# A kernel that streams weights through a ring: four places instead of five, one more weight pair on chip, and two PSUM accumulators instead of three

## The chip, the core and the metric

The kernel runs on one core of a Trainium2 chip. Its work is spread over engines with queues of their own: TensorE (PE; PEld are its weight loads), VectorE (DVE), ScalarE (ACT), GpSimd (POOL) and SyncE (SP, which here only issues DMAs). Each engine takes its instructions in the order in which the program gives them, and waits at an instruction until the semaphores that it needs have come. SBUF is the memory on chip that operands are read from, PSUM the one that TensorE writes its results to, and DRAM lies off chip. The metric is the device time of one execution in microseconds (us); lower is better.

## The reference

Two independent results stand side by side in the output. The first is a convolution layer (`A`); it is done in the kernel's first stages, which the change leaves alone. The second (`B`) is a recurrence over 64 segments of 32 tokens. Eight memory rows are carried from one segment to the next, so that no segment can begin before the one ahead of it has ended:

```python
for s in range(n_seg):                                   # 64 segments, seg_len 32
    xs = x[:, s * seg_len:(s + 1) * seg_len, :]
    h = jnp.concatenate([mem, xs], axis=1)               # 8 + 32 rows of 1024
    q = jnp.einsum('btd,dhe->bhte', h, Wq)               # 32 heads of 128
    k = jnp.einsum('btd,dhe->bhte', h, Wk)
    v = jnp.einsum('btd,dhe->bhte', h, Wv)
    scores = jnp.einsum('bhqe,bhke->bhqk', q, k) * scale
    p = _softmax(jnp.where(mask, scores, -1e9), axis=-1)
    o = jnp.einsum('bhqk,bhke->bhqe', p, v)
    o = jnp.einsum('bhte,hed->btd', o, Wo)
    mem = o[:, :M, :]                                    # M = 8
    outs.append(o[:, M:, :])
```

Each of `Wq`, `Wk`, `Wv`, `Wo` has 1024 x 4096 numbers of two bytes, so every segment uses 32 MB of weights.

## The kernel before

**Weight pairs.** The weights are cut into 64 pairs; a pair is a tile of 128 partitions x 2 x 1024 bf16, 512 KB or 4 KB in each partition. `("qk", g, kc)` holds rows 128 kc and on of `Wq` and `Wk` for the eight heads of group g (32 pairs), `("v", G, kc)` those of `Wv` for sixteen heads (16 pairs), and `("o", g, i)` two heads of `Wo` (16 pairs). They are kept in three ways, which `STREAM` (line 40) and `PARKED` (line 41) lay down. 45 pairs are resident in SBUF. 17 are streamed: each step fetches them from DRAM anew, into a ring of `RING` = 5 places of one pair each (line 697). Two are parked: they stay in PSUM, one tile of 128 x 1024 bf16 (2 KB in each partition) for each half pair (`park`, lines 669 and 670), and each step copies them into a place of the ring.

**The ring.** `done(key)` (line 725) is called when a streamed pair's last matmul has been issued. It takes the place for the next streamed pair in the order of use and issues that load on SP's queue (`place`, line 708). After the pairs that are keys of `PARKED` it gives the place to a parked pair instead, and `unpark` (line 716) copies that pair's first half with ACT (line 719) and its second half with DVE (line 720). `unpark` is called twice in a step: after the first half of group 0's q/k projection, and after group 0's transposes. A load of a pair waits for the matmuls that last read the place, and the loads behind it on SP's queue wait with it.

**One step.** The loop over 64 segments (line 908) is written out by hand, and this order is that of every engine's queue. Four groups u0 to u3 of eight heads go through these parts:

- `qk_part`: 32 matmuls accumulate q and k of one group, eight pairs with four matmuls each, into one PSUM tile of 128 x 512 fp32. `qk_out` (line 757) lets ACT cast it to `qks`.
- `tr_a` (line 783): four transposes on PE, then two ACT copies and one POOL copy to `QK`.
- `scores` (line 806): 20 small matmuls, then two DVE operations. `softmax` (line 828): two exponentials on ACT, then four DVE operations. `blocks` (line 845): four copies to `PB`, on DVE ("D") or ACT ("A").
- `v_part` (line 761): 32 matmuls for sixteen heads into `vacc`; `v_out` (line 772) is an ACT cast.
- `pv` (line 854): four matmuls into `otacc`; ACT casts the 32 rows of the segment to `OT` (line 863), DVE the other eight columns to `OL` (line 865).
- `wo` (line 869): 32 matmuls of one group into `Y`, which all four groups share.

`qkacc`, `vacc`, `otacc` and `yacc` are all tiles of the pool `ps_a` with three buffers (line 701): an accumulator waits for whoever read the one three before it. With the four park tiles, and one tile of `ps_ts` for the transposes and the scores, eight PSUM tiles of 2 KB in each partition are in use.

At the end of a step ACT casts `Y` (line 985), PE transposes its memory rows, and DVE writes them into the next `hT`, which every projection of the next step reads. POOL stores the outputs and loads the next `VB`.

**Order around the change.** Groups 2 and 3 go as follows (lines 944 to 970): the second half of u2's projection and its cast; `pv` of u0; `blocks` of u1; the first two pairs of u3's projection; u2's transposes; four more pairs; u2's scores and softmax; the last two pairs and the cast; then, in turns, one pair of v's second half, `pv` of u1, `blocks` of u2, one pair of v, u3's transposes, three pairs of v, u3's scores, softmax, the last three pairs of v, the cast of v, and `wo` of u0.

**Ahead of the loop** the resident pairs are loaded during the convolution stages, as SBUF comes free, the streamed q/k and output pairs are copied in DRAM into the shape of a pair (`relay`), and the parked halves are brought into PSUM through two rounds of transposes (lines 669 to 692). Nine output pairs are loaded in the first step (`first_loads`). In the last step the streamed output pairs are loaded once more, into places of resident pairs that are no longer needed (line 940). After the loop, four long accumulations (`pl`, line 1003) work out the outputs of the last eight rows of all segments.

Of the kernel before, what the change touches and what calls it, by code (L numbers as in the profile page):

```python
# [9 lines left out]
BF = mybir.dt.bfloat16  # L10
F32 = mybir.dt.float32
# [4 lines left out]
PSUM = bass.MemoryType.PSUM  # L16
# [5 lines left out]
def fused_kernel(ctx: ExitStack, tc, q, k, v, shift_k, ssm_k, ssm_D, outa, x, mem0, Wq, Wk, Wv, Wo, outb, n_seg):  # L22
# [11 lines left out]
    nc = tc.nc  # L34
# [3 lines left out]
    scale = 128.0 ** -0.5  # L38
    RING = 5
    STREAM = {"qk": ((2, 5), (3,), (2, 6), (2, 6)), "v": ((0, 3, 5), (1, 5)), "o": ((2,), (1,), (0, 3), (2,))}  # L40
    PARKED = {("qk", 0, 2): ("v", 0, 1), ("v", 0, 3): ("qk", 1, 6)}

    msched = tc.manual_schedule()
# [624 lines left out]

    ps_park = cw_.enter_context(tc.tile_pool(name="b_ps_park", bufs=1, space=PSUM))
    park = {key: [ps_park.tile([128, 1024], BF, name=f"park{key[1]}_{n}") for n in range(2)] for key in parked}  # L670

    park_s = stv.tile([128, 4, 1024], BF, tag="stv", name="park_s")
    halves = [(key, n) for key in parked for n in range(2)]
    assert rows.at >= 160
# [10 lines left out]
    for i, (key, n) in enumerate(halves):  # L685
        tw = ps_p.tile([128, 1024], BF, tag="pp", name="park_t")
        for c in range(8):
            nc.tensor.transpose(tw[:, c * 128:(c + 1) * 128], park_w[i][:, c * 128:(c + 1) * 128], ident[:])
        nc.vector.tensor_copy(park_s[:, i, :], tw[:])
        rows.half(2, "AD")  # L690
        for c in range(8):
            nc.tensor.transpose(park[key][n][:, c * 128:(c + 1) * 128], park_s[:, i, c * 128:(c + 1) * 128], ident[:])
    while rows.at < 192:
# [6 lines left out]
    pp = ExitStack()  # L700
    ps_a = pp.enter_context(tc.tile_pool(name="b_ps_a", bufs=3, space=PSUM))
    ps_ts = pp.enter_context(tc.tile_pool(name="b_ps_ts", bufs=1, space=PSUM))

    placed = {}
    to_copy = []
    todo = [key for s in range(n_seg) for key in streamed if key[0] != "o" or s < n_seg - 1]

    def place():

        if todo:  # L710
            key = todo.pop(0)
            t = ring.tile([128, 2, 1024], BF, tag="wring", name="wring")
            nc.sync.dma_start(t[:], Wst[key])
            placed.setdefault(key, []).append(t[:])

    def unpark():
        while to_copy:
            key, t = to_copy.pop(0)
            nc.scalar.copy(t[:, 0, :], park[key][0][:])  # L719
            nc.vector.tensor_copy(t[:, 1, :], park[key][1][:])  # L720

# [23 lines left out]
    def qk_part(u, kcs):  # L745
        if kcs[0] == 0:
            u.qk = ps_a.tile([128, 512], F32, tag="a", name="qkacc")
        for kc in kcs:
# [105 lines left out]
    def pv(u, s):  # L854
# [9 lines left out]
        to = OL[:] if s + 1 < n_seg else OLs[:, s]  # L864
        nc.vector.tensor_copy(to[:, 8 * u.g:8 * u.g + 8, :].rearrange("e (c i) r -> e i c r", i=2), ov[:, :, :, 32:40])
        if u.g == 3 and s + 1 < n_seg:
# [41 lines left out]
    for s in range(n_seg):  # L908
# [46 lines left out]
        qk_out(u3)  # L955
        v_part(1, range(0, 1))
        pv(u1, s)
        blocks(u2, "DDDD")
        v_part(1, range(1, 2))
        tr_a(u3)  # L960
        v_part(1, range(2, 5))
        S = scores(u3)
# [117 lines left out]
```

## Time and profile before

| what | value |
|---|---|
| time, median of 3 runs | 2148.29 us (2145.75 to 2157.45) |
| the profiled execution's own time | 2154.46 us |
| its span, from the first to the last instruction | 2152.6 us |
| granted TensorE clock, mean | 0.972 |
| PE, DVE, ACT, POOL busy | 1720.4, 1117.8, 921.1, 419.9 us |
| moved by DMA | 728.63 MB, 338 GB/s over the span |
| end of the first step (end of the cast of `Y`) | 454.5 us |
| end of the last step | 2083.1 us |
| mean step between these two, 63 steps | 25.85 us |
| final stage, after the last step | 69.5 us |

The page of the profile tells for each engine how long it was busy, in 40 slices of the span how busy it was and what the DMA engines moved, and for groups of instructions of one line how long one took, how long the engine had sat idle just before, and what ended that. The list of waits sums who waited for whom. The timeline lists instructions in the order of time. The step is worked out from the trace: the ends of the 64 instructions of line 985.

### The profile page before, as it was taken

What the parts mean: (1) busy time and instruction counts of PE and PEld (TensorE: products, weight loads), DVE (VectorE), ACT (ScalarE), POOL (GpSimd) and SP (SyncE); (2) the same over time, 40 slices, a digit from 0 to 9 for tenths busy, and PEclk for the clock granted to TensorE, in tenths of its full rate; (3) what the DMA queues carried; (4) which work ended last, traced back from release to release, by engine and by line L of the source; (5) the groups of instructions that cost most, each with busy time, mean ns of one, the idle gap of its engine ahead of it and who ended that gap; (6) DMA issues with size and microseconds to landing.
All of it is one profiled execution on the core that took longest, in us unless ns stands there. A gap on an engine that the chain in (4) does not pass through costs nothing. (4 is left out here: it accounts for less than half of the span.)

```text
span 2152.6 us, 74044 instructions
## 1 busy us (share of the span) xinstructions
PE 1720.4 (80%) x30514; PEld 895.9 (42%) x30514; DVE 1117.8 (52%) x3364; ACT 921.1 (43%) x2282; POOL 419.9 (20%) x1023
## 2 busy tenths in 40 slices
PE   4788987777887887788788888888888878788879
PEld 2332232334443444444444444444444444444448
DVE  6895842245554555555455555555555545555530
ACT  4546741134444444444444444444444444444430
POOL 4003630011111111111111221111111111221110
PEclk8999999889999999999999999999999999999999
DMA  7798969699999999999999999999999999999990
GB/s 238 287 337 312 360 236 355 215 364 360 364 374 323 363 372 368 354 354 352 337 368 369 373 352 372 369 364 365 361 354 367 363 346 375 366 369 371 367 321 22
DMA packets 267375, 728.63 MB, mean 338 GB/s; under 512 B 64751, under 2 KB 75903, under 8 KB 266525
## 3 DMA queue, kind: packets, MB, share of 16 engines
q1 hardware_dynamic: 241294, 687.24, 86.9%
q0 software_dynamic: 15520, 22.06, 3.3%
q10 hardware_dynamic: 10224, 14.62, 1.9%
q8 instruction: 239, 3.92, 0.7%
q14 instruction: 98, 0.80, 0.1%
HBM read 673.52 MB, written 56.56 MB: 339 GB/s over the span
## 5 line engine op out<-in xcount | busy, mean ns | idle before, releaser
L753 PE MATMUL qkacc<-Wqk,hT 128*32 128x512 bf16 x4096 | 339.5, 384 | 0.0
L753 PEld LDWEIGHTS <-hT 128*32 128x32 bf16 x8192 | 185.9, 96 | 241.9 <-issue 92.1
L874 PEld LDWEIGHTS <-OT 128*32 128x32 bf16 x8192 | 210.2, 96 | 108.9 <-issue 59.2
L874 PE MATMUL yacc<-Wo,OT 128*32 128x256 bf16 x5632 | 237.1, 274 | 16.7 <-ACT OT L863 14.7
L753 PE MATMUL qkacc<-wring,hT 128*32 128x512 bf16 x2048 | 207.5, 394 | 32.8 <-DMA wring<-Wstqk 26.5
L767 PE MATMUL vacc<-wring,hT 128*32 128x512 bf16 x1536 | 143.0, 387 | 100.2 <-DMA wring<-in_B_Wv_dram 98.4
L720 DVE COPY wring<-park 128x1024 bf16<-128x1024 bf16 x128 | 88.6, 692 | 242.3 <-PE vacc L767 164.0
L767 PE MATMUL vacc<-Wv,hT 128*32 128x512 bf16 x2560 | 209.8, 382 | 0.0
L767 PEld LDWEIGHTS <-hT 128*32 128x32 bf16 x4096 | 111.3, 95 | 226.4 <-issue 152.4
L833 ACT ACTIVATE P<-S 128x128 bf16<-128x128 f32 x256 | 71.1, 278 | 314.0 <-DVE S L825 233.5
L789 ACT COPY QK<-tp 128x256 bf16<-128x256 bf16 x256 | 95.4, 373 | 237.2 <-PE tp L780 237.2
L788 POOL COPY QK<-qkb 128x64 bf16<-128x64 bf16 x256 | 61.4, 240 | 652.9 <-PE tp L780 487.3
L753 PE MATMUL qkacc<-Wearly,hT 128*32 128x512 bf16 x2048 | 166.4, 403 | 18.5 <-DVE hT L894 17.9
L852 DVE COPY PB<-P 32x160 bf16<-32x160 bf16 x896 | 173.7, 194 | 10.6
L837 DVE TENSOR_REDUCE sm<-P 128x4 f32<-128x256 bf16 x256 | 107.5, 420 | 130.3 <-ACT P L834 130.3
L719 ACT COPY wring<-park 128x1024 bf16<-128x1024 bf16 x128 | 130.7, 1021 | 103.8 <-PE qkacc L753 100.8
L759 ACT CAST qks<-qkacc 128x512 bf16<-128x512 f32 x256 | 150.8, 589 | 28.8 <-PE qkacc L753 23.3
L874 PE MATMUL yacc<-wring,OT 128*32 128x256 bf16 x2520 | 126.4, 274 | 36.2 <-DMA wring<-Wsto 35.2
L863 ACT CAST OT<-otacc 128x256 bf16<-128x256 f32 x256 | 98.4, 384 | 126.8 <-PE otacc L859 126.8
L989 POOL DMA_DIRECT2D out_dram<-Y_sb x256 | 129.1, 511 | 89.9 <-ACT Y_sb L985 87.9
L824 DVE TENSOR_REDUCE mx<-S 128x4 f32<-128x160 f32 x256 | 83.2, 325 | 107.3 <-PE S L821 102.4
L780 PE MATMUL tp<-ident,qks 128*128 128x128 bf16 x1024 | 102.1, 222 | 42.6 <-ACT qks L759 39.3
(216 smaller groups left out, 2827.1 us busy)
## 6 DMA issues: line engine op xcount, KB each, us to landing
wring<-Wstqk SPq DMA_DIRECT2D x448, 512.0 KB, 6.3
wring<-in_B_Wv_dram SPq DMA_DIRECT2D x320, 512.0 KB, 6.7
wring<-Wsto SPq DMA_DIRECT2D x315, 512.0 KB, 6.0
SK<-s_sb SPq DMA_DIRECT2D x8, 1024.0 KB, 7.0
SU<-s_sb SPq DMA_DIRECT2D x8, 1024.0 KB, 6.7
QKBd<-stq ACTq DMA_DIRECT2D x4, 2048.0 KB, 10.9
Kg<-SK SPq DMA_DIRECT2D x16, 512.0 KB, 6.9
Ug<-SU SPq DMA_DIRECT2D x16, 512.0 KB, 7.5
```

Source lines behind the costliest of these rows:

```text
L719: nc.scalar.copy(t[:, 0, :], park[key][0][:])
L720: nc.vector.tensor_copy(t[:, 1, :], park[key][1][:])
L753: nc.tensor.matmul(u.qk[p0:p0 + 32, :], lhsT=hT[:, kc, :], rhs=w[:, t, c2 * 512:(c2 + 1) * 512], start=(kc == 0), stop=(kc == 7), tile_pos ...
L759: nc.scalar.copy(u.qks[:], u.qk[:])
L767: nc.tensor.matmul(vacc[0][32 * c:32 * c + 32, :].rearrange("p (n x) -> p n x", n=2), lhsT=hT[:, kc, :], rhs=w[:, :, c * 256:(c + 1) * 256 ...
L780: nc.tensor.transpose(tp[:, j * 128:(j + 1) * 128], src[:, j * 128:(j + 1) * 128], ident[:])
L789: nc.scalar.copy(u.QT.rearrange("e (c j) r -> e c j r", c=2), tv[:, 0])
L837: nc.vector.tensor_reduce(out=sm[:], in_=Pv.rearrange("p b x k -> p x b k"), op=ALU.add, axis=AX.XY)
L852: (nc.vector if by[c] == "D" else nc.gpsimd).tensor_copy(to, src)
L863: nc.scalar.copy(u.OT[:].rearrange("e (c i) q -> e i c q", i=2), ov[:, :, :, 0:32])
L874: nc.tensor.matmul(Y[32 * dq:32 * dq + 32, 0:256], lhsT=u.OT[:, hh, 0:32], rhs=w[:, hh % 2, dq * 256:(dq + 1) * 256], start=(u.g == 0 and ...
L989: nc.gpsimd.dma_start(outb[32 * s:32 * s + 24, dq * 256:(dq + 1) * 256], Y_sb[32 * dq + 8:32 * dq + 32, :])
```

## The change

Four things change together.

- `RING` is 4 instead of 5, and one pair more is resident (46). `STREAM` is laid out anew: of q/k 8 pairs are streamed instead of 7 (group 2 has pairs 1, 4 and 6 instead of 2 and 6), of v 4 instead of 5 (`("v", 0, 0)` is resident), of the output 4 instead of 5 (group 2 has pair 1 instead of 0 and 3). That makes 16 streamed pairs instead of 17.
- One of the 16, `HALF` = `("o", 3, 2)`, is streamed by half. Its first half is parked in PSUM in a fifth park tile; `place` loads the second half alone, 256 KB, and a third call of `unpark`, after `pv` of u2, lets ACT copy the first half.
- The three shared accumulators become two pools with one tile each: `ps_q` for `qkacc` and `yacc`, and `ps_a` for `vacc` and `otacc`. With five park tiles and `ps_ts` these are eight again.
- The copy to `OL` moves from DVE to ACT. In the order of the loop the first two pairs of v's second half move: `pv` of u1 comes straight after u3's cast, then `blocks` of u2 and u3's transposes, and then four pairs of v at a stretch, u3's scores and softmax, and the other four.

The park pool is closed ahead of the final stage.

```diff
-    RING = 5
-    STREAM = {"qk": ((2, 5), (3,), (2, 6), (2, 6)), "v": ((0, 3, 5), (1, 5)), "o": ((2,), (1,), (0, 3), (2,))}
+    RING = 4
+    STREAM = {"qk": ((2, 5), (3,), (1, 4, 6), (2, 6)), "v": ((3, 5), (1, 5)), "o": ((2,), (1,), (1,), (2,))}
     PARKED = {("qk", 0, 2): ("v", 0, 1), ("v", 0, 3): ("qk", 1, 6)}
+    HALF = ("o", 3, 2)
...
-    ps_park = cw_.enter_context(tc.tile_pool(name="b_ps_park", bufs=1, space=PSUM))
-    park = {key: [ps_park.tile([128, 1024], BF, name=f"park{key[1]}_{n}") for n in range(2)] for key in parked}
+    pk = ExitStack()
+    ps_park = pk.enter_context(tc.tile_pool(name="b_ps_park", bufs=1, space=PSUM))
+    park = {key: [ps_park.tile([128, 1024], BF, name=f"park{key[0]}{key[1]}_{n}") for n in range(1 + (key != HALF))]
+            for key in parked + [HALF]}
...
-    halves = [(key, n) for key in parked for n in range(2)]
+    halves = [(key, n) for key in parked for n in range(2)] + [(HALF, 0)]
...
-        nc.vector.tensor_copy(park_s[:, i, :], tw[:])
+        nc.vector.tensor_copy(park_s[:, i % 4, :], tw[:])
...
-    ps_a = pp.enter_context(tc.tile_pool(name="b_ps_a", bufs=3, space=PSUM))
+    ps_q = pp.enter_context(tc.tile_pool(name="b_ps_q", bufs=1, space=PSUM))
+    ps_a = pp.enter_context(tc.tile_pool(name="b_ps_a", bufs=1, space=PSUM))
...
             t = ring.tile([128, 2, 1024], BF, tag="wring", name="wring")
-            nc.sync.dma_start(t[:], Wst[key])
+            if key == HALF:
+                nc.sync.dma_start(t[:, 1, :], Wst[key][:, 1, :])
+                to_copy.append((key, t))
+            else:
+                nc.sync.dma_start(t[:], Wst[key])
             placed.setdefault(key, []).append(t[:])
...
             nc.scalar.copy(t[:, 0, :], park[key][0][:])
-            nc.vector.tensor_copy(t[:, 1, :], park[key][1][:])
+            if key != HALF:
+                nc.vector.tensor_copy(t[:, 1, :], park[key][1][:])
...
-            u.qk = ps_a.tile([128, 512], F32, tag="a", name="qkacc")
+            u.qk = ps_q.tile([128, 512], F32, tag="q", name="qkacc")
...
-        nc.vector.tensor_copy(to[:, 8 * u.g:8 * u.g + 8, :].rearrange("e (c i) r -> e i c r", i=2), ov[:, :, :, 32:40])
+        nc.scalar.copy(to[:, 8 * u.g:8 * u.g + 8, :].rearrange("e (c i) r -> e i c r", i=2), ov[:, :, :, 32:40])
...
         qk_out(u3)
-        v_part(1, range(0, 1))
         pv(u1, s)
         blocks(u2, "DDDD")
-        v_part(1, range(1, 2))
         tr_a(u3)
-        v_part(1, range(2, 5))
+        v_part(1, range(0, 4))
         S = scores(u3)
...
         softmax(u3, S)
-        v_part(1, range(5, 8))
+        v_part(1, range(4, 8))
         u2.v = u3.v = v_out()
-        Y = ps_a.tile([128, 512], F32, tag="a", name="yacc")
+        Y = ps_q.tile([128, 512], F32, tag="q", name="yacc")
         wo(u0, Y)
...
         pv(u2, s)
+        unpark()
         blocks(u3, "DDAA")
...
     pp.close()
+    pk.close()
```

More of the change, by code (lines that the diff above doesn't have):

```diff
@@ L688, in fused_kernel @@
             nc.tensor.transpose(tw[:, c * 128:(c + 1) * 128], park_w[i][:, c * 128:(c + 1) * 128], ident[:])
-        nc.vector.tensor_copy(park_s[:, i, :], tw[:])
+        nc.vector.tensor_copy(park_s[:, i % 4, :], tw[:])
         rows.half(2, "AD")
         for c in range(8):
-            nc.tensor.transpose(park[key][n][:, c * 128:(c + 1) * 128], park_s[:, i, c * 128:(c + 1) * 128], ident[:])
+            nc.tensor.transpose(park[key][n][:, c * 128:(c + 1) * 128], park_s[:, i % 4, c * 128:(c + 1) * 128], ident[:])
     while rows.at < 192:
```

## The prediction

> **What bounds the kernel now.** I read the page first: the 40 slices, the DMA queues and the issues. Under the slices stand the group of the parked copies and the issues.
>
> ```profile
> PEclk8999999889999999999999999999999999999999
> DMA  7798969699999999999999999999999999999990
> GB/s 238 287 337 312 360 236 355 215 364 360 364 374 323 363 372 368 354 354 352 337 368 369 373 352 372 369 364 365 361 354 367 363 346 375 366 369 371 367 321 22
> ...
> q1 hardware_dynamic: 241294, 687.24, 86.9%
> ...
> L719 ACT COPY wring<-park 128x1024 bf16<-128x1024 bf16 x128 | 130.7, 1021 | 103.8 <-PE qkacc L753 100.8
> ...
> wring<-Wstqk SPq DMA_DIRECT2D x448, 512.0 KB, 6.3
> wring<-in_B_Wv_dram SPq DMA_DIRECT2D x320, 512.0 KB, 6.7
> wring<-Wsto SPq DMA_DIRECT2D x315, 512.0 KB, 6.0
> ```
>
> From the ninth slice on, which is the loop, the DMA engines are at 9 tenths or more and the TensorE clock is near full. The reader should look at the DMA row, not at the busy shares of the engines (PE 80%). The stretch of the 63 steps alone, 454.5 to 2083.1 us, was asked next; behind the times stand the busy times of PE, PEld, DVE, ACT and POOL, then clock, DMA share and GB/s:
>
> ```profile
> 454.50:2083.10 1628.60, 1318.61 (x27466) 696.31 (x27466) 845.53 (x2897) 715.84 (x1953) 307.99 (x881) 0.99 0.98 362
> ```
>
> DMA is busy for 0.98 of it, so 25.3 us of a step of 25.85 us. Then the list of waits, to see whether PE feels it:
>
> ```profile
> PE vacc L767 <- DMA wring<-in_B_Wv_dram: 98.4, 151, 8.6
> PE yacc L874 <- DMA wring<-Wsto: 35.2, 71, 1.3
> PE qkacc L753 <- DMA wring<-Wstqk: 26.5, 40, 3.4
> ```
>
> PE waits for ring loads for 160.1 us, 2.5 us a step. So the step without those waits is about 25.85 - 2.5 = 23.35 us. That is a chain of small dependences (PE, ACT and DVE in turns), and it lies only 2 us below the transfers. Both floors matter. Last, the timeline of one step, around the hand-offs that the change touches:
>
> ```profile
> 1015.23 0.61 PE L753 MATMUL qkacc<-Wqk,hT 128*32 128x512 bf16 x8
> 1015.88 0.59 ACT L759 CAST qks<-qkacc 128x512 bf16<-128x512 f32 x1
> 1016.52 0.40 PE L780 MATMUL tp<-ident,qks 128*128 128x128 bf16 x4 [0.68 <-ACT qks L759]
> ...
> 1019.58 0.59 ACT L759 CAST qks<-qkacc 128x512 bf16<-128x512 f32 x1
> 1020.05 0.40 ACT L863 CAST OT<-otacc 128x256 bf16<-128x256 f32 x1
> ...
> 1020.55 0.83 PE L767 MATMUL vacc<-Wv,hT 128*32 128x512 bf16 x12
> ...
> 1024.36 0.37 ACT L863 CAST OT<-otacc 128x256 bf16<-128x256 f32 x1 [0.54 <-PE otacc L859]
> 1025.03 0.66 ACT L850 COPY PB<-P 32x160 bf16<-32x160 bf16 x2 [0.30 <-DVE P L842]
> ```
>
> Twice PE stands before u's transposes until ACT has cast `qks`. Ahead of the first of these waits it does two pairs of u3's projection.
>
> **The change part by part.**
>
> *Transfers.* A step streams 15.5 pairs instead of 17, that is 1.5 x 0.524 = 0.786 MB less. At the loop's 362 GB/s this is 2.17 us. By the queue's own row (687.24 MB in 0.869 x 2152.6 = 1871 us) it is 2.14 us. Half a pair moves in packets half as long; the trace's packets of 2048 bytes took 94 ns on average (39,582 of them, nearly all ahead of the loop), those of 4096 bytes in the loop 174 ns. So the half costs 8 packets on each of 16 engines x 94 = 0.75 us instead of 0.70. I take 2.1 us off, which leaves 23.2 us of transfers. With the 0.5 us that they are not busy now, the transfers alone would allow 23.7 us.
>
> *Two accumulators.* Of the hand-offs between the users of one PSUM tile, most have other work in between (u0's cast, the second projection: `v_part` and four transposes lie between). Two have not. First, u3's opening two pairs, at 1015.23, would now wait for u2's cast, which ends at 1016.47. They took the place of a wait, so what is lost is their issue time, eight matmuls, 0.43 us (so much lies, at 1004.16 and 1004.60 of the same timeline, between the starts of eight such matmuls and of the next ones). u2's transposes and everything behind them on PE come that much later. Second, `vacc` now waits for ACT's `OT` and `OL` of u1. `OT` ends at 1020.45, `OL` adds about 0.1 behind it (ACT's next starts 0.11 us before the last one's end; its duration I put at 0.22 us, between the 0.19 of the 128 x 32 exponential and the 0.40 of the 128 x 256 cast). So v starts near 1020.65 instead of 1020.55, and u3's scores stand behind 16 matmuls instead of 12 (another 0.2). That is 0.3 us. The four matmuls more that follow hide beside the scores' DVE and ACT work.
>
> *OL to ACT.* Each goes off DVE (0.19) and onto ACT (0.1 to 0.24). Between u1 and u3 DVE runs nearly without a gap, so DVE gains 0.1 a group there; ACT's are behind `OT`, and what waits for them is `vacc` (counted) and POOL's `OLd`, which nobody needs before the end. Between -0.2 and +0.3 us a step; I take 0.
>
> *The third unpark.* One ACT copy of 128 x 1024 bf16, 1.02 us by line 719's row, between `OT` of u2 and ACT's two copies for `PB` of u3. Those stand at 1025.03 to 1025.69; behind `OT` (begun at 1024.36), `OL` and the copy they would end near 1024.36 + 0.26 + 0.11 + 0.91 + 0.66 = 1026.3. `pv` of u3 needs them, and behind it in ACT's queue are `OT` of u3 and the cast of `Y`. In this step `pv` came at 1026.97, after a stall for transfers; without that it would come near 1026.1 to 1026.4. So it costs 0 to 0.3 us; I take 0.2. `wo` of u3 needs the copied half later still. Its place is free by then: v's pair 5 has been used.
>
> *The ring.* Four places instead of five: at most four transfers are outstanding, and while a parked pair or a pair in use holds one, three. Loads landed 6.0 to 6.7 us after issue (median), with five. The least was this:
>
> ```profile
> DMA to landing us min/median/max: 3.2/6.3/9.6
> ```
>
> 6.3 us is 4.5 times the 1.4 us that one pair takes (2.14 / 1.5), so most of it is queueing behind the other places, which falls with their number. Three outstanding need 4.2 us at this rate, above the 3.2 of an empty queue. So I expect full rate most of the time, and some loss where three pairs of group 2 come close together (pairs 1, 4 and 6 within about 1.3 us of PE's work, against 2.8 us of transfers). Bounds: 0 to 1 us a step; I take 0.2.
>
> *Moved instructions.* `pv` of u1 moves ahead of one pair of v; its `PB` blocks ended well before (the DVE copies run behind u1's softmax, and u3's shift of 0.43 gives them more time). SP's queue has one load less in a step, none moved past another. POOL's instructions stay, its `OLd` waits for ACT instead of DVE.
>
> *Ahead of and behind the loop.* One more round through PE and DVE to park the fifth half: 16 transposes and a copy of 0.69 us, +1 us. In the first step ten output pairs are loaded instead of nine, and 1.5 fewer are streamed: -0.7 us. In the last step one load of 512 KB less stands before the last gather, which the final stage waits for: -1.4 us. Together -1 us.
>
> *Sum for a step.* The dependence floor goes from 23.35 to 23.35 + 0.43 + 0.3 + 0.2 = 24.3 us if every wait is on the path. The transfer floor is 23.7 us. Where PE now waits for a load, an added wait of PE costs nothing, so the two do not add. But neither is the dependence floor fully on the path: u3's scores are followed by a DVE that only just becomes free. I take 24.05 us, between 23.7 (+0.2 for the ring) and 24.3. That is 1.8 us less, x 63 = 113 us, and 1 us outside: 114 us. The profiled execution, 2154.5 us by its own time (2.2 us more than its span), would become 2040 us. It lay 6.2 us above the median of the three runs; against that median, 2148.3 - 114 = **2034 us**.
>
> **The rivals.**
>
> *The waits add up* (0.19). Dependences and ring both cost their upper bounds: step 23.35 + 0.43 + 0.3 + 0.3 + 1.0 = 25.4 us, 2119 us, or anything from 24.5 us on. For it: 0.9 us is all that separates the floors. Against it: 2.5 us of DMA waits now cover much of that.
>
> *Accumulators must rotate* (0.05). If each hand-off exposed its cast, four of 0.59 us and four of `OT` with `OL` (0.61) would lie open, 4.8 us a step on 23.35: 28.1 us, +144 us, 2292 us. Against it speaks the timeline: two of the eight are uncovered, and ACT's cast of `qks` was a wait of PE before. The Trainium skill, Perfetto Trace Analysis, "Optimizing Tensor Performance", asks for just that: independent groups of matmuls should rotate through different PSUM banks, so that one's evacuation overlaps the next one's matmuls. No run yet shows this kernel with one bank per kind.
>
> *The ring starves the transfers* (0.05), the other side. If a load keeps taking 6.3 us with four places, because the time is latency and no queue, a place's turn is 6.3 + 0.4 (use) + 0.2 (issue) = 6.9 us. Sixteen such turns a step and two of parked pairs (about 2 us each) over four places are (110.4 + 4) / 4 = 28.6 us, +173 us: about 2320 us. It decides from 25.85 us on: (4 x 25.85 - 4) / 16 - 0.6 = 5.6 us to landing. Against it: 3.2 us was reached.
>
> *It frees nothing* (0.05): landings stay as late against their use, and the step stays at 25.7 to 26.0 us, 2139 to 2158 us.
>
> *More than forecast* (0.06): added waits hide wholly and the idle 0.5 us of the DMA engines goes: 23.2 us, 167 us less, 1980 us.
>
> **How the numbers follow.** The forecast has what is left, 0.60, with 2008 to 2062 us as its own range (23.65 to 24.5 us a step). For the range of 8 in 10 I add the waits that add up, as far as 2105 us (25.2 us a step, about 0.16 of their 0.19), and begin at 2008: outside lie 0.06 below, 0.03 + 0.05 + 0.05 + 0.05 above, together a little over 0.2, so I stretch the upper end to 2115 us. Within 0.5% (2137.5 to 2159 us) is about what a measurement of this kernel can tell from no change: 0.05. Faster is 0.60 + 0.19 + 0.06 = 0.85, slower 0.10.
>
> **What would show it.** In the loop's stretch: about 24 us a step, DMA share 0.95 or more, GB/s near 355, bytes down by some 50 MB. In the waits: PE on `wring` down to 0.5 to 1.3 us a step, a new wait of PE `qkacc` for ACT `qks` after `pv` of u0, of `vacc` for `OL`, and of `otacc` for `PB` on ACT. Issue to landing near 4.8 us. I am wrong if the DMA share falls below 0.9 with PE waiting for ACT (accumulators), or if it falls with landings still near 6 us (ring).

## The result and the profile after

The changed kernel takes 2241.18 us (median of 4 runs, 2236.54 to 2271.98), against 2147.02 us for the kernel before, measured beside it. The ratio is 1.0437, with a 95% interval of 1.0399 to 1.0474: it is 4.4% slower, where the prediction said 5.3% faster and gave 2115 us as the upper end of its range. The execution of 2271.98 us was in a slower state of the chip and is left out of the ratio.

The slices of the profile, the queue row and the issues of the changed kernel:

```profile
PEclk9999989799999999999999999999999999999999
DMA  7799888899999999999999999999999999999990
GB/s 254 271 350 351 295 293 288 291 309 316 319 316 307 319 309 314 326 314 314 319 306 313 312 314 305 330 312 306 312 319 308 308 309 311 317 320 316 316 326 22
...
q1 hardware_dynamic: 232510, 637.95, 83.2%
...
wring<-Wstqk SPq DMA_DIRECT2D x512, 512.0 KB, 5.6
wring<-in_B_Wv_dram SPq DMA_DIRECT2D x256, 512.0 KB, 5.6
wring<-Wsto SPq DMA_DIRECT2D x189, 512.0 KB, 5.4
wring<-Wsto SPq DMA_DIRECT2D x63, 256.0 KB, 5.4
```

The DMA row still shows nines all through the loop. The row under it does not: some 312 GB/s a slice where the kernel before had some 365. The queue moved 637.95 MB instead of 687.24, 49.3 less, as forecast. So there is less to move, and it is moved more slowly.

The stretch of the 63 steps between the ends of the first and the last cast of `Y` (start and end, length, busy time of PE, PEld, DVE, ACT and POOL with the number of instructions, granted clock, DMA share, GB/s):

```profile
450.50:2175.00 1724.50, 1313.03 (x27478) 716.55 (x27482) 828.09 (x2645) 809.19 (x2267) 301.63 (x881) 0.98 0.93 314
```

A step takes 27.37 us instead of 25.85. Over 63 steps that is +95.9 us; outside the loop 12.9 us were gained (the first step ends 4.0 us sooner, the final stage takes 60.6 us instead of 69.5). Together that is the +83.0 us between the spans, 2152.6 and 2235.6. The granted clock of the loop is 0.98 against 0.99 and PE's busy time is 5.6 us lower, so PE doesn't work longer. It waits longer, as the list of waits shows (in total, times, longest, in us):

```profile
PE vacc L776 <- DMA wring<-in_B_Wv_dram: 99.0, 68, 5.9
PE qkacc L762 <- DMA wring<-Wstqk: 94.5, 147, 2.9
PE tp L789 <- ACT qks L768: 61.0, 64, 2.0
PE yacc L883 <- DMA wring<-Wsto: 51.0, 70, 2.0
PE qkacc L762 <- ACT qks L768: 20.8, 58, 0.6
```

The three waits for ring loads make 244.5 us, against 160.1 us before: 3.82 us a step instead of 2.50, which is 1.32 us more where the step grew by 1.52. The two waits for ACT's cast `qks` are those of the accumulators: that of the transposes (`tp`) was 39.3 us before, that of the projection (`qkacc`) is new. What is added there is partly made up by other waits and by the 5.6 us that PE is busy for less, so the list alone does not split the loss. What the trace answers for line 721, which issues the loads of whole pairs, tells how long they took:

```profile
DMA to landing us min/median/max: 3.2/5.5/10.7
```

The median fell from 6.3 to 5.5 us. The prediction needed 4.8. The timeline of one step shows the waits in their places:

```profile
1003.91 0.40 PE L776 MATMUL vacc<-wring,hT 128*32 128x512 bf16 x4 [2.44 <-DMA wring<-in_B_Wv_dram]
...
1006.61 0.40 PE L762 MATMUL qkacc<-wring,hT 128*32 128x512 bf16 x4 [0.27 <-DMA wring<-Wstqk]
...
1007.89 0.40 PE L762 MATMUL qkacc<-wring,hT 128*32 128x512 bf16 x4 [0.67 <-DMA wring<-Wstqk]
...
1008.61 0.59 ACT L768 CAST qks<-qkacc 128x512 bf16<-128x512 f32 x1 [0.96 <-PE qkacc L762]
1009.25 0.61 PE L762 MATMUL qkacc<-Wqk,hT 128*32 128x512 bf16 x8 [0.35 <-ACT qks L768]
...
1012.53 0.59 ACT L768 CAST qks<-qkacc 128x512 bf16<-128x512 f32 x1
1013.18 0.40 PE L789 MATMUL tp<-ident,qks 128*128 128x128 bf16 x4 [1.03 <-ACT qks L768]
1013.57 0.40 PE L776 MATMUL vacc<-Wv,hT 128*32 128x512 bf16 x4
```

At 1003.91, 1006.61 and 1007.89 PE waits for the ring: the last streamed pair of v's first half and two pairs of group 2. At 1009.25 u3's projection waits for u2's cast, as foreseen. At 1013.18 u3's transposes wait 1.03 us for u3's cast: this wait stands in no step of the prediction.

### The profile page after: what moved, and what is told of

Its sections match the earlier page's. It is cut to its first block, busy times and chain, and to the rows that moved or that the text cites. A ratio compares the mean times of both kernels' runs of the same rounds, so it can differ in the third digit from the quotient of the medians.

```text
span 2235.6 us, 74244 instructions
## 1 busy us (share of the span) xinstructions
PE 1709.7 (76%) x30500; PEld 915.6 (41%) x30530; DVE 1100.6 (49%) x3109; ACT 1016.2 (45%) x2601; POOL 413.2 (18%) x1023
## 3 DMA queue, kind: packets, MB, share of 16 engines
q1 hardware_dynamic: 232510, 637.95, 83.2%
## 5 line engine op out<-in xcount | busy, mean ns | idle before, releaser
L762 PEld LDWEIGHTS <-hT 128*32 128x32 bf16 x8192 | 194.7, 97 | 339.7 <-issue 196.1
L762 PE MATMUL qkacc<-wring,hT 128*32 128x512 bf16 x2304 | 236.2, 398 | 99.7 <-DMA wring<-Wstqk 94.5
L883 PE MATMUL yacc<-Wo,OT 128*32 128x256 bf16 x6144 | 253.0, 276 | 21.4 <-ACT OT L872 21.0
L776 PE MATMUL vacc<-Wv,hT 128*32 128x512 bf16 x2816 | 247.3, 383 | 0.0
L776 PE MATMUL vacc<-wring,hT 128*32 128x512 bf16 x1280 | 128.3, 384 | 99.5 <-DMA wring<-in_B_Wv_dram 99.0
L776 PEld LDWEIGHTS <-hT 128*32 128x32 bf16 x4096 | 111.3, 96 | 202.9 <-issue 126.4
L762 PE MATMUL qkacc<-Wearly,hT 128*32 128x512 bf16 x2048 | 161.2, 392 | 18.4 <-DVE hT L903 17.9
L883 PE MATMUL yacc<-wring,OT 128*32 128x256 bf16 x2016 | 101.9, 276 | 52.6 <-DMA wring<-Wsto 51.0
L789 PEld LDWEIGHTS <-qks 128*128 128x128 bf16 x1024 | 59.5, 99 | 157.0 <-ACT qks L768 99.8
L851 DVE STREAM_TRANSPOSE P<-P 128x256 bf16<-128x256 bf16 x256 | 114.0, 445 | 8.8
```

The costliest lines, as they stand in the source:

```text
L762: nc.tensor.matmul(u.qk[p0:p0 + 32, :], lhsT=hT[:, kc, :], rhs=w[:, t, c2 * 512:(c2 + 1) * 512], start=(kc == 0), stop=(kc == 7), tile_pos ...
L776: nc.tensor.matmul(vacc[0][32 * c:32 * c + 32, :].rearrange("p (n x) -> p n x", n=2), lhsT=hT[:, kc, :], rhs=w[:, :, c * 256:(c + 1) * 256 ...
L789: nc.tensor.transpose(tp[:, j * 128:(j + 1) * 128], src[:, j * 128:(j + 1) * 128], ident[:])
L851: nc.vector.transpose(out=Pf, in_=Pf)
L883: nc.tensor.matmul(Y[32 * dq:32 * dq + 32, 0:256], lhsT=u.OT[:, hh, 0:32], rhs=w[:, hh % 2, dq * 256:(dq + 1) * 256], start=(u.g == 0 and ...
```

## The experiments

Two theories stood against each other. The ring theory (R): four places hold too few loads under way, so the transfers run slower, whatever the DMA engines' busy share says. The accumulator theory (A): the two accumulators, with the new order and `OL` on ACT, cost more than thought. All ratios are against the kernel before on the same chip. "Step" is the mean over the 63 steps of the profiled execution; the waits are the sums of its list of waits, divided by 64.

| kernel | ratio (95%) | step, us | PE waits for ring loads, us a step | GB/s | DMA share |
|---|---|---|---|---|---|
| before | 1 | 25.85 | 2.50 | 362 | 0.98 |
| after | 1.0437 (1.0399 to 1.0474) | 27.37 | 3.82 | 314 | 0.93 |
| four places alone | 1.1356 (1.1312 to 1.1400) | 30.57 | 6.01 | 307 | 0.89 |
| four places, one pair more on chip | 1.0439 (1.0359 to 1.0520) | 27.34 | 4.28 | 324 | 0.93 |
| after with five places | 1.0240 (1.0191 to 1.0289) | 26.68 | 2.94 | 342 | 0.96 |
| two accumulators alone | 1.0235 (1.0203 to 1.0266) | 26.49 | 2.45 | 353 | 0.98 |
| order alone | 1.0156 (1.0125 to 1.0186) | 26.27 | 2.44 | 356 | 0.98 |
| six places, one pair less on chip | 0.9924 (0.9893 to 0.9954) | 25.63 | 1.44 | 386 | 1.02 |
| pairs spread anew, five places | 0.9934 (0.9902 to 0.9966) | 25.56 | 2.28 | 367 | 0.99 |

**Four places alone.** One line of the kernel before.

```diff
-    RING = 5
+    RING = 4
```

> The kernel before with four ring places instead of five and nothing else (45 resident pairs, 17 streamed, three accumulators; 4 KB of SBUF stay unused). Theory R (the ring: with four places too few loads are under way, and the transfers slow down): a place's turn in the changed kernel is 4 x 27.37 / 18 = 6.08 us; here 19 turns a step share four places, so 19 x 6.08 / 4 = 28.9 us a step, about +190 us, ratio 1.09. Theory A (the two accumulators and ACT's added work make it slow): no change, ratio 0.99 to 1.01.

The step went to 30.57 us, 4.7 us more, at the same bytes a step. The stretch of the steps, and the waits:

```profile
451.60:2377.60 1926.00, 1437.59 (x27466) 732.51 (x27467) 844.73 (x2897) 716.11 (x1953) 302.69 (x881) 0.90 0.89 307
```

```profile
PE yacc L874 <- DMA wring<-Wsto: 159.6, 141, 3.4
PE vacc L767 <- DMA wring<-in_B_Wv_dram: 142.6, 121, 6.9
PE qkacc L753 <- DMA wring<-Wstqk: 82.5, 80, 6.6
```

PE's waits for the ring rose by 3.5 us a step, from 2.50 to 6.01. The granted clock of the loop fell to 0.90 too, and PE's busy time rose by 119 us (1.9 us a step); how much of the rest of the loss hangs on that, this run doesn't tell. R holds: a place is worth far more than the 0.2 us that the prediction gave it, and more even than R had expected.

**Four places and the new set of pairs, the old three accumulators, no half pair.**

```diff
-    RING = 5
-    STREAM = {"qk": ((2, 5), (3,), (2, 6), (2, 6)), "v": ((0, 3, 5), (1, 5)), "o": ((2,), (1,), (0, 3), (2,))}
+    RING = 4
+    STREAM = {"qk": ((2, 5), (3,), (1, 4, 6), (2, 6)), "v": ((3, 5), (1, 5)), "o": ((2,), (1,), (1,), (2,))}
```

> The kernel before with four places and the new spread (46 resident pairs, 16 streamed), but three accumulators, OL on DVE, the old order and no parked half. Theory R: 18 turns on four places as in the changed kernel, with half a pair more to move: 27.4 to 27.9 us a step, ratio 1.045 to 1.06. Theory A: the ring's gain without its cost, 24 us a step, ratio 0.945.

The stretch of its steps, from 2 us after its start to 2 us before its end:

```profile
452.00:2170.00 1718.00, 1344.83 (x27410) 708.36 (x27403) 849.76 (x2895) 721.53 (x1951) 303.30 (x878) 0.97 0.93 324
```

This is as slow as the whole change, with none of its accumulators, and within what R had expected (its 1.045 lies inside the interval). One pair less to stream and the new spread win back 3.2 of the 4.7 us that the place cost; 1.49 us stay.

**The change with five places.** The place comes back, and `("v", 0, 0)` is streamed again to make room; 16.5 pairs.

```diff
-    RING = 4
-    STREAM = {"qk": ((2, 5), (3,), (1, 4, 6), (2, 6)), "v": ((3, 5), (1, 5)), "o": ((2,), (1,), (1,), (2,))}
+    RING = 5
+    STREAM = {"qk": ((2, 5), (3,), (1, 4, 6), (2, 6)), "v": ((0, 3, 5), (1, 5)), "o": ((2,), (1,), (1,), (2,))}
```

> The changed kernel with five places again, paid for with the pair (v, 0, 0), which is streamed as before: 16.5 pairs streamed, half a pair less than the kernel before. Theory R: the loads run at the 362 GB/s of before, so 25.85 x 9.03 / 9.29 MB = 25.1 us a step, -46 us, ratio 0.98. Theory A: it keeps the changed kernel's waits and has more to load, so ratio 1.04 or more.

1.024 is neither theory's number. With the place back, and half a pair more to stream, 2.0 of the 4.4% are gone and 2.4% stay. So A has a part too, and the next kernel shows its size.

**Two accumulators alone**: the change with five places, the old `STREAM` and no half pair. What is left of the change is `ps_q` and `ps_a`, the new order and `OL` on ACT.

```diff
-    RING = 4
+    RING = 5
...
-    HALF = ("o", 3, 2)
+    HALF = None
```

> The kernel before with the two accumulators, the new order of v and pv and the copy to OL on ACT, but with five places, the old spread and no parked half. Theory R: the transfers bound the step as before, so 0 to +0.3 us a step, ratio 1.00 to 1.01. Theory A: most of the loss, +1 to +1.5 us a step, ratio 1.03 to 1.04.

The stretch of its steps, and its waits for ACT's cast:

```profile
451.00:2120.10 1669.10, 1309.71 (x27466) 709.53 (x27466) 829.37 (x2645) 742.93 (x2205) 306.78 (x881) 0.98 0.98 353
```

```profile
PE tp L789 <- ACT qks L768: 62.2, 62, 1.2
PE qkacc L762 <- ACT qks L768: 39.6, 64, 1.1
```

The ratio of 1.0235 lies between the two theories. The step is 0.64 us longer, and PE still waits 2.45 us a step for ring loads, as before (2.50). So the waits for the ring did not shrink to make room for the added ones.

**What the two chains of dependences are without transfers.** In both kernels no streamed pair is loaded in the loop; its matmuls read a resident pair instead, so the work of the engines stays and the weights are others. In the kernel after, the half pair keeps its place, its load and its ACT copy. The core of both edits:

```diff
     def pair(key):
-        return res[key][:, :, :] if key in res else placed[key].pop(0)
+        if key in res:
+            return res[key][:, :, :]
+        if key in placed and placed[key]:
+            return placed[key].pop(0)
+        m, g, i = key
+        return res[next(k for k in resident if k[:2] == (m, g))][:, :, :]
...
-        else:
-            place()
```

> The kernel before without the loop's ring loads: a streamed pair's matmuls read a resident pair of the same kind and group, so the result is another, but every matmul, cast and parked copy stays. Measures the chain of dependences that is left when no load is waited for. The prediction put it at 23.35 us a step (25.85 less PE's 2.5 us of waits): 1990 us, ratio 0.93. If PE's waits hide more than the list shows, 22.5 us, 1940 us.

> The changed kernel without the ring loads, in the same way (the half pair keeps its place, its load of 256 KB and ACT's copy). Measures what the two accumulators, the copy to OL on ACT and the copy of the parked half add to the chain. The prediction: 23.35 + 0.43 + 0.3 + 0.2 = 24.3 us a step, 0.95 us above the floor of before. Theory A (waits of the accumulators explain the whole loss): 1.5 us or more above. Theory R (the ring alone): 0.5 us or less.

The ratios are 0.8941 (0.8887 to 0.8994) and 0.9126 (0.9068 to 0.9184). The stretches of the steps, first without the transfers of the kernel before, then of the one after:

```profile
431.70:1849.70 1418.00, 1229.44 (x27466) 677.32 (x27466) 830.31 (x2897) 710.36 (x1953) 305.51 (x881) 1.00 0.09 23
```

```profile
436.00:1895.40 1459.40, 1218.89 (x27466) 698.26 (x27466) 817.04 (x2645) 795.85 (x2268) 308.16 (x881) 1.00 0.12 33
```

By 63 steps that is 22.51 and 23.16 us (from the ends of the steps): the added waits cost 0.65 us of the chain, where the prediction's terms made 0.43 + 0.3 + 0.2 = 0.93 (0.95 after rounding to 24.3). Waits of PE, first in the kernel before without transfers, then in the one after:

```profile
PE tp L783 <- ACT qks L762: 63.2, 123, 1.2
```

```profile
PE tp L795 <- ACT qks L771: 66.2, 64, 1.4
PE qkacc L765 <- ACT qks L771: 51.3, 64, 1.2
PE otacc L874 <- ACT PB L865: 18.5, 63, 0.3
```

The transposes wait as long in all as before, once a step instead of twice; what is new is u3's projection behind `qks` (51.3 us) and `pv` behind `PB` (18.5 us, 0.29 us a step). The second of these is the third unpark's, which the kernel with two accumulators alone does not have. So of the 0.65 us the accumulators, order and `OL` make between 0.36 and 0.65, and the 0.64 us that they cost under full transfers with five places are no less than that.

**Which part of the accumulators.** First, two `ps_q` tiles in the kernel with two accumulators, so that `qkacc` and `yacc` rotate again:

```diff
-    ps_q = pp.enter_context(tc.tile_pool(name="b_ps_q", bufs=1, space=PSUM))
+    ps_q = pp.enter_context(tc.tile_pool(name="b_ps_q", bufs=2, space=PSUM))
```

> The run with the two accumulators alone (ratio 1.0235), with a second tile for the q/k accumulator and Y, so that u3's projection need not wait for u2's cast; v and pv still share one tile, OL stays on ACT, and the order is the new one. If the wait of u3's projection is what costs, 0.4 us a step come back: ratio 1.005 to 1.015. If it is the shared tile of v and pv, or ACT's added copies, it stays at 1.02 to 1.025.

1.0222 (1.0193 to 1.0251), against 1.0235 with one tile: no difference that the intervals tell. The wait of u3's projection (39.6 us) is gone from the list, but the transposes now wait 82.3 us for the cast instead of 62.2. (The profiled execution is the fastest of this kernel's five, so its step is not compared.) Second, the new order in the kernel before, with its three accumulators and `OL` on DVE:

```diff
         qk_out(u3)
-        v_part(1, range(0, 1))
         pv(u1, s)
         blocks(u2, "DDDD")
-        v_part(1, range(1, 2))
         tr_a(u3)
-        v_part(1, range(2, 5))
+        v_part(1, range(0, 4))
```

> The kernel before with the new order alone: pv of u1, blocks of u2 and u3's transposes ahead of v's second half; three accumulators, OL on DVE. If the order is what the two accumulators cost (eight matmuls that stood in the wait for u3's cast come after it), about 0.4 us a step: ratio 1.01 to 1.02. If the shared tiles cost it, 1.00.

The wait of the transposes for the cast, first in the kernel before, then in this one:

```profile
PE tp L780 <- ACT qks L759: 39.3, 65, 3.8
```

```profile
PE tp L780 <- ACT qks L759: 83.4, 93, 1.6
```

The ratio is 1.0156 (1.0125 to 1.0186), as expected if the order is what costs. The wait of the transposes grew by 44.1 us, 0.69 us a step; the step grew by 0.42. Two pairs of v, eight matmuls, stood between u3's cast and u3's transposes; in the new order only `pv` of u1 does. Third, `OL` alone, in both directions: on ACT in the kernel before, and back on DVE in the kernel with two accumulators.

```diff
-        nc.vector.tensor_copy(to[:, 8 * u.g:8 * u.g + 8, :].rearrange("e (c i) r -> e i c r", i=2), ov[:, :, :, 32:40])
+        nc.scalar.copy(to[:, 8 * u.g:8 * u.g + 8, :].rearrange("e (c i) r -> e i c r", i=2), ov[:, :, :, 32:40])
```

> The kernel before with OL on ACT and nothing else. If ACT's queue is on the path, ratio 1.01; by the prediction (0 us, bounds -0.2 to +0.3 us a step) 1.00.

> The run with the two accumulators alone (1.0235), with OL back on DVE. If ACT's four added copies a step are what costs, ratio 1.005 to 1.01; if not, 1.02 or more.

On ACT in the kernel before: 1.0005 (0.9977 to 1.0034), nothing. On DVE with two accumulators: 1.0485 (1.0451 to 1.0520), with a wait that the others don't show, in its list of waits:

```profile
PE vacc L776 <- DVE OL L874: 52.6, 63, 0.8
```

So with a shared `vacc` and `otacc` the copy is cheaper on ACT: PE waits up to 0.8 us for DVE to get to it. Beside the 2.35% of the two accumulators the order alone costs 1.56%; the rest is not split further, and that the parts add is taken, not shown. The Trainium skill (Perfetto Trace Analysis, "Optimizing Tensor Performance") wants independent groups of matmuls to rotate through PSUM banks. Here giving `qkacc` a second bank changed nothing measurable in the time, since the wait came back at the transposes, and the new order cost 1.56% with all three banks in place.

**Is it the number of DMAs, or the time of each?** Each whole load was split in two, so that twice as many were under way in the same places: by partitions, first in the kernel after, then in the kernel before, and by half pairs with all 128 partitions in the kernel before.

```diff
-                nc.sync.dma_start(t[:], Wst[key])
+                for p in (0, 64):
+                    nc.sync.dma_start(t[p:p + 64], Wst[key][p:p + 64])
```

> The changed kernel, each whole load issued as two DMAs of 64 partitions: the bytes under way stay, the number of DMAs under way doubles. If the transfers slow down because few DMAs are under way, the rate comes back from 314 to 350 GB/s or more, 25 us a step, ratio 0.98. If it is the bytes under way (four places of 512 KB), it stays at 27.3 us, ratio 1.03 to 1.05.

> The kernel before with the same split of each load. If the number of DMAs under way sets the rate, 362 GB/s becomes 380 or more, 24.6 us a step, ratio 0.965. If the bytes do, ratio 1.00.

```diff
-            nc.sync.dma_start(t[:], Wst[key])
+            for n in range(2):
+                nc.sync.dma_start(t[:, n, :], Wst[key][:, n, :])
```

> The kernel before with each load issued as two DMAs of half a pair, each over all 128 partitions, in packets of 2048 bytes; the split by partitions had slowed every packet and so did not answer the question. If the number of DMAs under way sets the rate, the gain outweighs the shorter packets: ratio 0.97 to 0.99. If the bytes under way set it, the packets' overhead is left (8 x 2 x 92 ns instead of 8 x 174 ns, +6%): 26.5 to 27.2 us a step, ratio 1.03 to 1.05.

The two by partitions took 1.3717 (1.3656 to 1.3777) and 1.4701 (1.4624 to 1.4778). The one by halves took 1.0644 (1.0610 to 1.0677). All three are above everything that was expected of them. The stretches of the steps of the second and the third (its last 9 us left out):

```profile
464.10:3083.50 2619.40, 1739.35 (x27466) 718.32 (x27466) 853.99 (x2897) 735.44 (x1954) 300.43 (x881) 0.77 0.99 225
```

```profile
452.00:2200.00 1748.00, 1373.76 (x27286) 701.79 (x27284) 839.10 (x2881) 709.58 (x1943) 306.19 (x879) 0.96 0.98 335
```

Packets of 4096 bytes took 286 ns (median) in the split by partitions, 159 in the kernel before: the DMA share is 0.99 at 225 GB/s. The Trainium skill (DMA: Bandwidth & Descriptors, "Rules for kernel authors") advises against two transfers to disjoint halves of the partitions, because both run on the same engines one after the other. Here they were far worse than one after the other, 225 GB/s against 362. The split by halves halves the packets, which took 93.6 ns on average, 187 for two against 173 for one of 4096 bytes. More DMAs in the same places made nothing faster here. Both ways of splitting lengthened the packets' time for a byte as well, so they do not test the number alone.

**More places, and the spread alone.** If R is right, a sixth place should pay even for one pair more to stream. The new spread was tried alone with five places, at 17 pairs as before, and both together.

```diff
-    RING = 5
-    STREAM = {"qk": ((2, 5), (3,), (2, 6), (2, 6)), "v": ((0, 3, 5), (1, 5)), "o": ((2,), (1,), (0, 3), (2,))}
+    RING = 6
+    STREAM = {"qk": ((2, 5), (3,), (2, 6), (2, 6)), "v": ((0, 3, 5), (1, 3, 5)), "o": ((2,), (1,), (0, 3), (2,))}
```

> The kernel before with a sixth place, paid for with the pair (v, 1, 3), which is streamed too: 18 pairs a step. If another place is worth what the fifth was (4.65 us a step between the run with four places and the kernel before) less one pair's transfer, it becomes faster: ratio 0.92 to 0.95. If the transfers are near their best rate with five places (373 GB/s with five loads under way), 9.82 MB at 375 GB/s are 26.2 us: ratio 1.00 to 1.015.

```diff
-    STREAM = {"qk": ((2, 5), (3,), (2, 6), (2, 6)), "v": ((0, 3, 5), (1, 5)), "o": ((2,), (1,), (0, 3), (2,))}
+    STREAM = {"qk": ((2, 5), (3,), (1, 4, 6), (2, 6)), "v": ((3, 5), (1, 5)), "o": ((2,), (1,), (0, 3), (2,))}
```

> The kernel before with five places, 45 resident and 17 streamed pairs, but the changed kernel's spread of q/k and v: (v, 0, 0) resident, and three pairs of group 2 streamed (1, 4, 6) instead of two. If the spread matters, three loads close together are waited for: 26.3 us a step or more, ratio 1.015 or more. If the ring evens it out, ratio 0.99 to 1.005.

```diff
+    RING = 6
+    STREAM = {"qk": ((2, 5), (3,), (1, 4, 6), (2, 6)), "v": ((3, 5), (1, 3, 5)), "o": ((2,), (1,), (0, 3), (2,))}
```

> The two faster runs together: six places, 44 resident and 18 streamed pairs, with (v, 0, 0) resident and three pairs of group 2 and of v's second half streamed. If their gains add, 0.9924 x 0.9934 = 0.986. If the transfers already run at their best rate with six places (386 GB/s; 9.82 MB take 25.4 us), no better than 0.99.

Six places: 2127.51 us, 0.9924. The stretch of its steps, and its loads:

```profile
448.60:2063.10 1614.50, 1311.99 (x27466) 694.89 (x27466) 847.78 (x2897) 714.64 (x1954) 306.70 (x881) 0.98 1.02 386
```

```profile
DMA to landing us min/median/max: 3.3/7.0/10.5
```

It moves one pair more in a step and is 0.8% faster, at 386 GB/s: less than a whole further place was expected to bring (0.92 to 0.95), and better than transfers already at their best rate (1.00 or more). The spread alone: 2127.43 us, 0.9934. Both gains are below 1%, with intervals that leave out 1. Together they took 1.0038 (1.0014 to 1.0062), with 1.35 us of ring waits a step but 26.0 us for the step: the gains don't add. Against the spread alone PE waits 0.93 us a step less for the ring, but the transposes wait 118.0 us for the cast `qks` instead of 41.0, and those of the next step's inputs 44.8 us for the load of `H` instead of 10.7. Why these waits grow stays open, as does why the spread gains.

The spread kernel is also the fairest partner of the one with four places and the new set of pairs: the two differ in one place and in group 2's output pairs (0 and 3 streamed, or 1 alone). The step is 25.56 us with the place and 27.34 without it, so a pair on chip instead of a ring place cost 1.78 us.

## Why the prediction was wrong, point by point

**Transfers.** The bytes were right: 49.3 MB less, where some 50 were forecast. What was wrong is what they are divided by. "At the loop's 362 GB/s" took a rate for a constant that depends on the ring. From the issue and landing of each load in the trace one can count the loads under way on average (for one load in eight whose landing the trace doesn't tell, halfway was taken) and the mean time of one:

| kernel | under way | mean landing, us | GB/s |
|---|---|---|---|
| four places alone | 3.18 | 5.70 | 307 |
| after | 3.23 | 5.50 | 314 |
| four places, new set of pairs | 3.39 | 5.77 | 324 |
| after with five places | 3.90 | 6.11 | 342 |
| two accumulators alone | 4.05 | 6.31 | 353 |
| before | 4.20 | 6.39 | 362 |
| pairs spread anew, five places | 4.23 | 6.34 | 367 |
| six places | 4.96 | 7.05 | 386 |

The order by loads under way is the order by rate, in all eight. The rate is tied to the two columns by bookkeeping: for the kernel after, 16 loads move 15.5 pairs of 0.524 MB, 0.508 MB each, so 3.23 x 0.508 / 5.50 = 298 GB/s, and the loop's other transfers add about 17. So the table alone does not tell what leads to what. With two accumulators and `OL` on DVE, five places and the loads of before, PE's longer waits by themselves brought 3.84 loads under way and 341 GB/s. That a place leads to the rate is shown by the kernels in which the place alone was changed, or the place and one pair. Nor is the number of loads all of it: with three and with four under way the kernel before moved 340 and 362 GB/s, the kernel after 313 and 335.

**The ring: the step that failed.** "Three outstanding need 4.2 us at this rate, above the 3.2 of an empty queue. So I expect full rate most of the time", at 0.2 us a step and at most 1. It measured 1.78 us a step with the saved pair already taken off (25.56 to 27.34), and 4.72 us where no pair was saved. Two things were wrong in it. Loads under way are not three at least but 3.2 on average, two for 12% of the time of the kernel after, when the rate was about 270 GB/s. And the time of a load doesn't shrink to its share of the queue: from 4.20 to 3.23 loads, 23% fewer, the mean landing fell by 14% only (6.39 to 5.50). How much of it isn't queueing is seen in the kernel after without its other loads. There the half loads had the DMA engines nearly to themselves (issues: KB each, median us to landing):

```profile
wring<-Wsto SPq DMA_DIRECT2D x63, 256.0 KB, 3.4
```

Eight packets of about 84 ns (median) on each engine make 0.7 us; the other 2.7 us went by with almost nothing ahead in the queue. By the same sum a load of 512 KB has eight packets of 159 ns, 1.3 us, so of the prediction's 3.2 us some 1.9 are, by estimate, not packet time. The prediction took most of the 6.3 us to landing for queueing that falls with the number of places.

**The DMA share read as work.** "DMA is busy for 0.98 of it, so 25.3 us of a step": it wasn't a floor. The same engines moved 386 GB/s with six places. Packets of 4096 bytes have the same median in the kernels before and after, 159 ns, but the mean rose from 173 to 188, and the share of packets above 250 ns from 3.6% to 7.3% (2.3% with six places). The share counts stretched packets as busy time, so 0.93 at 314 GB/s looks nearly full. Of the prediction's signs the one for the accumulators, a DMA share "below 0.9", was not reached, at 0.93; "0.95 or more", GB/s near 355 and landing near 4.8 us were all missed, and its sign for the ring, a falling share "with landings still near 6 us", came close with 0.93 and 5.5 us.

**The two accumulators.** The mechanisms were there, the terms were partly mis-sized: the cast of u2 before u3's first pairs shows as the new wait of 0.35 us at 1009.25 (term 0.43). `vacc` behind `OT` and `OL` and the scores behind 16 matmuls made 0.3 in the sum; what the reorder really costs is u3's transposes, which now come at once behind u3's cast (order alone: +0.42 us a step). The whole, with the third unpark, is 0.65 us on the chain where 0.93 was taken.

**"Where PE now waits for a load, an added wait of PE costs nothing, so the two do not add": the second step that failed.** With five places they add in full: at most +0.65 us with no transfers, +0.64 us with all of them, at the same 2.45 us of ring waits. The argument would hold if transfers went on while PE waits for ACT and if what they gain could be used later. But the ring holds five pairs. Once its places are full, a wait of PE keeps places from coming free, and fewer loads are under way (4.20 in the kernel before, 4.05 with two accumulators). The traces bear this out: from its landing to its first matmul a pair stands in its place for 0.44 us on average in the kernel before and for 0.69 us with two accumulators (loads whose landing is known). No run took it apart further. With four places this step is not tested by itself: the whole change is only 0.03 us a step slower than the kernel with its four places and its pairs alone (27.37 and 27.34), and there PE's waits for the ring did fall, from 4.28 to 3.82. Either the added waits were covered there in part, as the prediction had it, or the half pair paid for them; both fit. The chain itself was read too long, 23.35 us against 22.51 measured, since 25.85 less the ring waits is not the step without transfers.

**Third unpark, `OL` to ACT, half pair.** `OL` on ACT costs nothing where the accumulator isn't shared (1.0005), as taken. PE waits for `PB` behind the third unpark for 18.5 us in all without transfers, 0.3 us a step, as bounded; in the changed kernel itself for 0.3 us in all. The half pair: if the parts add, they make 25.85 + 1.49 + 0.64 = 27.98 us where the whole change takes 27.37, so the half pair would have returned about 0.6 us. That is not shown: no run has four places and two accumulators without it, and with five places it returned nothing (26.68 us with it and the new set of q/k and output pairs, 26.49 without).

**Outside the loop.** -1 us was forecast, -12.9 came: 4.0 by the end of the first step, for which no run gives a cause, and 8.9 in the final stage (69.5 to 60.6 us). All seven kernels with loads in the loop that have four places or the new spread took 60.4 to 61.5 us there, the others with such loads 67.4 to 69.7. The traces tell what differs. In the kernel before the final stage began with a wait for the gather of `OLd`:

```profile
PE pl L1003 <- DMA Wearly<-OLd: 6.7, 1, 6.7
```

That gather was issued 11.0 us before the end of the last step there and 17.7 us before it in the changed kernel, where PE does not wait for it at all; this holds for all seven. So the prediction's -1.4 us for this gather had the right place and too small a size. The rest of the 8.9 us is in the stage's matmuls, 55.5 us instead of 57.9. Why the gather is issued so much sooner stays open.

**The rivals.** "The ring starves the transfers" had a chance of 0.05 and was nearest: it decides from 5.6 us to landing, and 5.5 was measured. By its own formula 5.5 us give (16 x 6.1 + 4) / 4 = 25.4 us; the step took 27.37, so each of the 18 turns lasts another 4 x 1.97 / 18 = 0.44 us. The formula has no time in which a landed pair waits for its use; in the trace that is 0.55 us on average. "The waits add up" (0.19) named 25.4 us a step, with the ring at its bound of 1.0 us; the ring cost 1.78. The rival that accumulators must rotate (28.1 us) is out at its size: the two accumulators cost 0.64 us a step with five places, not 4.8, and a second tile in `ps_q` changed nothing that could be measured. A second tile in `ps_a` was not tried.

## What to carry to other kernels

Read a transfer-bound stretch by GB/s and by the loads under way, not by the DMA share: a share of 0.93 to 1.02 went with anything from 314 to 386 GB/s here, and with 225 where the loads were split by partitions. Before a ring place is traded for a resident tile, work out what one place less does to the loads under way and to the rate, with the measured landing time falling by less than the queue; in this kernel the trade the other way round, one place more and one pair more to stream, gained 0.8% with the old spread of pairs and lost 1% with the new one (1.0038 against 0.9934). And don't count on waits for transfers to cover a wait that is added to the dependence chain: here, with five places, the two costs added, since a place comes free only after its pair has been used.

## What the runs showed of the hardware

- A load of 512 KB as two DMAs of 64 partitions ran at 224 to 225 GB/s instead of 314 to 362, with packets of 286 ns instead of 159 (medians, 4096 bytes each). Nothing in the trace says why.
- A load of 256 KB with almost nothing else on the DMA engines took 3.4 us from issue to landing, one of 512 KB among the loop's other loads 5.5 to 7.0 us on average.
- With fewer loads under way the packets did not get shorter but some of them much longer: 2.3% of those of 4096 bytes took over 250 ns with 4.96 loads under way, 3.6% with 4.20, 7.3% with 3.23. The cause is open.
- The granted clock of the loop fell where PE waited most for loads: 0.90 with four places alone and 0.77 with loads split by partitions in the kernel before, against 0.98 and 0.99 in the kernels after and before. Waits for loads are not all of it: with two accumulators and `OL` on DVE it was 0.95, at 2.39 us of such waits a step. No run tells what leads to what.
